# Attention and maxout FFN on one core: the order of every engine's work from a list scheduler in the source instead of the framework's

## The chip, the cores and the metric

One core of a Trainium2 chip runs the kernel. The metric is the device time of one execution in microseconds (us); the median of the runs is compared.

## The reference

Four batches, eight heads, 768 positions, head size 64. Each query sees only the keys that fall to the same of 16 centroids; the attention result, heads side by side, goes through a feed-forward layer whose hidden value is the largest of three products.

```python
q_assign = np.argmax(np.einsum('bhsd,hcd->bhsc', q_n, c_n), axis=-1)
k_assign = np.argmax(np.einsum('bhsd,hcd->bhsc', k_n, c_n), axis=-1)
mask = q_assign[:, :, :, None] == k_assign[:, :, None, :]
scores = np.where(mask, scale * np.matmul(q, k.transpose(0, 1, 3, 2)), -1000000000.0)
attn = np.exp(scores - np.max(scores, axis=-1, keepdims=True))
attn = attn / (np.sum(attn, axis=-1, keepdims=True) + 1e-09)
x = np.matmul(attn, v)                       # then (3072, 512), heads side by side
h = np.maximum(np.maximum(x @ w1, x @ w2), x @ w3)
out = h @ w_out
```

Operands are split into a high and a low 16-bit half, so each product is three or more TensorE passes.

## The kernel before

The unit of attention is a score tile: 128 queries of one head against all 768 keys. There are 192, numbered in this text from 1. `scores` makes one: four TensorE matmuls into a PSUM tile `big` (L505, L507), a scaled maximum on VectorE (L510), the exponential on ScalarE with the row's sum (L513), its high half on ScalarE (L515), its low half on VectorE for even steps and on GpSimd for odd ones (L517), and a transposing DMA of both halves into `pt` (L518), issued by SyncE like every other DMA of the kernel. On odd steps the exponential goes to a buffer `e` in SBUF, on even ones it stays in `big`.

Six tiles (three of each head of a pair) make a visit; 32 visits in all, 8 for each batch. After a visit `av_sums` (L526, L527, L532) spreads the inverse row sums into a `big` tile, `av` multiplies the transposed weights with V into it (36 matmuls, L540), and `x_split` (L551 to L558) scales it into the input `x16` of the FFN. For batches after the first the scaling (L553) needs `vrel`, which `v_common` (L309) forms when all four pairs of V of that batch have been scaled.

Four visits complete the 384 rows of one FFN block; there are eight. `hidden` makes 18 groups of 12 matmuls (L585), each taken from PSUM by ScalarE or VectorE (L595, L597); `outp` makes three groups of 18 (L619), taken by ScalarE (L628) and stored (L630). Both use PSUM tiles `one`.

Before its first visit a pair of heads is prepared: its load (L372), maxima (L381), a small power-of-two matmul (L390), the split into halves (L407 to L417), cluster scores on TensorE (L444, L448), copies between partitions (L424 to L427), and the one-hot cluster rows: a transpose, an addition, a subtraction and selections (L455 to L480), then four row DMAs into `qk` (L484). V is prepared in L344 to L352. In the first 230 us or so, 24 blocks of FFN weights are also loaded (L187), put together from halves (L194, L196), scaled by a power of two found with a small matmul (L102 to L111; the matmul is L106) and split (L205 to L207).

Buffers that matter here: three `big` and two `one` PSUM tiles; in SBUF four `hl`, three `pt`, two `e`, two `wd`, four `stage`, one `xs`.

The order: the source calls these functions step by step, gives each call a priority (`at_prio`, `spread`, `paced`, `put`) and some edges (`issue_after`), and the framework's scheduler, with a timing model of its own, orders single instructions by priority. The result is a fixed order on each engine; at run time an engine's head instruction waits for its semaphores, and what stands behind it waits too.

Of the kernel before, what the change touches and what calls it, by code (L numbers as in the profile page):

```python
# [9 lines left out]
F32R = mybir.dt.float32r  # L10
# [10 lines left out]
CSC = 2.0**10  # L21


@with_exitstack
def kernel(
# [11 lines left out]

# [13 lines left out]
    NG = QT // G  # L62

    cpool = ctx.enter_context(tc.tile_pool(name="const", bufs=1))
    sb = ctx.enter_context(tc.tile_pool(name="sb", bufs=2))
    ps_big = ctx.enter_context(tc.tile_pool(name="ps_big", bufs=3, space=PSUM))
    ps_one = ctx.enter_context(tc.tile_pool(name="ps_one", bufs=2, space=PSUM))

    def big():
        return ps_big.tile([P, 2 * 512], F32, tag="big", name="big")  # L70

    def one():
        return ps_one.tile([P, 512], F32, tag="one", name="one")

    def stage():
        return sb.tile([P, S], F32, tag="stage", name="stage", bufs=4)

    fp = [ctx.enter_context(tc.tile_pool(name="ffn", bufs=2))]
    tctx = ExitStack()
    tp = tctx.enter_context(tc.tile_pool(name="first", bufs=1))  # L80
    ident = cpool.tile([P, P], F32, name="ident")
    make_identity(nc, ident)
    ident16 = cpool.tile([P, P], BF16, name="ident16")
    nc.gpsimd.tensor_copy(ident16, ident)
    rank = cpool.tile([P, C], F32, name="rank")
    for c in range(C):
        nc.gpsimd.memset(rank[:, c : c + 1], float(C - c))
    onehot2 = cpool.tile([P, S // 32, 2, C], F16, name="onehot2")
    cw = cpool.tile([P, H, P], F16, name="cw")
    nc.gpsimd.memset(cw, 0.0)  # L90
    ksel = cpool.tile([P, 1], F32, name="ksel")
    for g in range(4):
        nc.gpsimd.memset(ksel[32 * g : 32 * g + 32], float(g & 1))
    hsel = cpool.tile([P, 2], F32, name="hsel")
# [3 lines left out]

    def pow2_scale(cols, name, p=None):

        m = sb.tile([P, 1], F32, tag="sc_m", name="sc_m", bufs=2)
        nc.vector.tensor_reduce(m, cols, axis=AX.X, op=ALU.max)  # L102
        nc.vector.tensor_scalar_max(m, m, 1e-30)
        nc.vector.tensor_scalar(m.bitcast(I32), m.bitcast(I32), 0x7F800000, None, op0=ALU.bitwise_and)
        a = one()[:, 0:P]
        nc.tensor.matmul(a, m.bitcast(BF16)[:, 1:2].broadcast_to([P, P]), ident16, start=True, stop=True)  # L106
        p = cpool.tile([P, 1], F32, name=f"p_{name}") if p is None else p
        s = sb.tile([P, 1], F32, tag="sc_s", name="sc_s", bufs=6)
        nc.vector.tensor_reduce(p, a, axis=AX.X, op=ALU.max)  # L109
        nc.vector.reciprocal(s, p)  # L110
        nc.vector.tensor_scalar_mul(s, s, 2.0**14)  # L111
        return p, s
# [3 lines left out]
    last = {}  # L116

    def behind(what, f, *args):
        with tc.issue_after(last[what].ins):
            f(*args)  # L120


    def load_centroids():
        c_sb = sb.tile([P, D], F32, tag="c_sb", name="c_sb", bufs=1)
        nc.sync.dma_start(out=c_sb, in_=cent)
        return c_sb

    def centroids(c_sb):
        warm = cpool.tile([P, 1], F32, name="warm")
        nc.vector.memset(warm, 1.0)  # L130
        nc.scalar.activation(warm, warm, AF.Sqrt)
        sq = tp.tile([P, D], F32, name="sq")
        ss = cpool.tile([P, 1], F32, name="c_ss")
        nc.vector.tensor_tensor(sq, c_sb, c_sb, op=ALU.mult)
        nc.vector.tensor_reduce(ss, sq, axis=AX.X, op=ALU.add)
        y0 = cpool.tile([P, 1], F32, name="c_y0")
        nc.scalar.activation(y0, ss, AF.Sqrt)
        nc.scalar.activation(warm, ss, AF.Exp)
        yr = cpool.tile([P, 1], F32, name="c_yr")
        nc.vector.tensor_scalar_max(yr, y0, 1e-18)  # L140
        nc.vector.reciprocal(yr, yr)
        nc.vector.tensor_tensor(yr, ss, yr, op=ALU.mult)
        nc.vector.tensor_tensor(yr, y0, yr, op=ALU.add)
        nc.vector.tensor_scalar(yr, yr, 0.5, 1e-6, op0=ALU.mult, op1=ALU.add)
        nc.vector.reciprocal(yr, yr)
        c2 = tp.tile([P, 2, D], F32, name="c2")
        cb = c_sb.rearrange("p (a d) -> p a d", a=1).broadcast_to([P, 2, D])
        nc.vector.tensor_scalar_mul(c2, cb, yr)
        t = one()
        nc.tensor.transpose(t[:, 0:P], c2.rearrange("p a d -> p (a d)"), ident)  # L150
        tv = t[:, 0:P].rearrange("p (h c) -> p h c", c=C)
        cv = cw.rearrange("p (r i) x -> p r i x", i=2)
        tv = tv.rearrange("p (r i) c -> p r i c", i=2)
        parts = []
        for a in range(2):
            rows = slice(D * a, D * a + D)
            for i in range(2):
                at = D * i + 32 * a
                parts.append((tv[rows, :, i, :], cv[rows, :, i, at : at + C], cv[rows, :, i, at + C : at + 2 * C]))
        for x, hi, lo in parts:  # L160
            last["cw_hi"] = nc.scalar.activation(hi, x, AF.Copy, scale=CSC)
        for x, hi, lo in parts:
            last["cw_lo"] = nc.vector.scalar_tensor_tensor(lo, x, CSC, hi, op0=ALU.mult, op1=ALU.subtract)

    JA = 4
# [34 lines left out]

    def w_units(wp, jt):
        mx = wmx[:, jt : jt + 1]  # L210
        n = CT * P
        got = {}

        def load(i):
# [599 lines left out]
```

## Time and profile before

| | us |
|---|---|
| three runs | 858.05, 856.37, 858.34 |
| median | 858.05 |
| the profiled execution's own time | 856.58 |
| its span | 854.8 |
| PE busy (matmuls) | 708.7 |
| DVE, ACT, POOL busy | 556.0, 474.2, 456.1 |
| granted TensorE clock over the span | 0.928 |

The span is the time between the first and the last recorded event of that execution, 1.78 us less than its own time. Engines: PE is TensorE, DVE VectorE, ACT ScalarE, POOL GpSimd, SP SyncE. L505 is line 505 of the kernel before. A row of waits reads: engine, tile and line that waited, what ended the wait, the total in us, how often, the longest.

### The profile page before, as it was taken

What the parts mean: (1) busy time and instruction counts of PE and PEld (TensorE: products, weight loads), DVE (VectorE), ACT (ScalarE), POOL (GpSimd) and SP (SyncE); (2) the same over time, 40 slices, a digit from 0 to 9 for tenths busy, and PEclk for the clock granted to TensorE, in tenths of its full rate; (3) what the DMA queues carried; (4) which work ended last, traced back from release to release, by engine and by line L of the source; (5) the groups of instructions that cost most, each with busy time, mean ns of one, the idle gap of its engine ahead of it and who ended that gap; (6) DMA issues with size and microseconds to landing.
All of it is one profiled execution on the core that took longest, in us unless ns stands there. A gap on an engine that the chain in (4) does not pass through costs nothing.

```text
span 854.8 us, 13244 instructions
## 1 busy us (share of the span) xinstructions
PE 708.7 (83%) x4629; PEld 390.5 (46%) x4629; DVE 556.0 (65%) x1150; ACT 474.2 (55%) x837; POOL 456.1 (53%) x448
## 2 busy tenths in 40 slices
PE   2254452667989999998987899999798999999997
PEld 1122121333555455554544455555345555555563
DVE  6967858879588486368675685569768764665020
ACT  5657555776754546564663566665457465566201
POOL 1267467498676544255873654366666643454221
PEclk9995665797999999999989999999899999999999
DMA  6698795899588766678977966688978976667300
GB/s 235 127 218 178 182 222 113 185 228 201 125 178 168 154 118 127 138 140 164 188 150 155 190 133 125 146 166 159 194 158 162 154 138 136 124 112 119 86 1 37
DMA packets 329154, 128.90 MB, mean 151 GB/s; under 512 B 304384, under 2 KB 315520, under 8 KB 329088
## 3 DMA queue, kind: packets, MB, share of 16 engines
q1 hardware_dynamic: 329088, 128.06, 72.4%
q8 instruction: 36, 0.59, 0.3%
q14 instruction: 30, 0.25, 0.1%
HBM read 31.49 MB, written 6.29 MB: 44 GB/s over the span
## 4 chain that ended last, share of the span: by engine, by line
PE 52%; DVE 16%; DMA 10%; POOL 9%; issue 7%; ACT 4%; SPq 1%; POOLq 0%; DVEq 0%; ACTq 0%
PE one L585 22%; PE one L619 10%; PE big L540 8%; DMA stage<-in_qk_dram 5%; PE big L505 4%; PE big L507 4%; DVE big L510 4%; PE big L532 2%; POOL hl L517 2%; DMA stage<-in_v_dram 2%; DMA wd<-in_moe_w_dram 2%; POOL qk L417 2%; DVE hl L517 2%; DVE wf L196 2%; DMA pt<-hl 1%
## 5 line engine op out<-in xcount | busy, mean ns | idle before, releaser
L517 POOL TENSOR_TENSOR hl<-e,hl 128x768 f16<-128x768 f32 x96 | 158.6, 1652 | 162.3 <-ACT hl L515 162.3
L510 DVE TENSOR_SCALAR_CACHE_REDUCE big<-big,nsc 128x768 f32<-128x768 f32 x192 | 193.8, 1019 | 63.3 <-PE big L507 61.7
L585 PE MATMUL one<-x,w16a 128*128 128x384 f16 x1152 | 207.7, 328 | 7.0 <-DVE vpow L109 3.2
L505 PE MATMUL big<-qk 128*128 128x512 f16 (+1 forms) x384 | 105.3, 358 | 65.8 <-ACT e L513 27.5
L513 ACT ACTIVATE big<-big,nm 128x768 f32<-128x768 f32 x96 | 83.9, 874 | 127.5 <-DVE big L510 103.3
L585 PEld LDWEIGHTS <-w16a 128*128 128x128 f16 x1152 | 110.8, 98 | 87.7 <-issue 18.0
L513 ACT ACTIVATE e<-big,nm 128x768 f32<-128x768 f32 x96 | 86.7, 903 | 74.7 <-DVE big L510 65.1
L540 PE MATMUL big<-pt,v 128*64 128x384 f16 x1152 | 118.6, 344 | 1.0 <-DMA pt<-hl 0.9
L507 PE MATMUL big<-qk 96*128 96x512 f16 (+1 forms) x384 | 107.0, 359 | 13.2 <-DMA qk<-cl_t 12.1
L517 DVE TENSOR_TENSOR hl<-big,hl 128x768 f16<-128x768 f32 x96 | 91.2, 950 | 33.7 <-ACT hl L515 33.7
L585 PE MATMUL one<-x,w16b 128*128 128x384 f16 x576 | 102.8, 329 | 0.0
L505 PEld LDWEIGHTS <-qk 128*128 128x128 f16 x384 | 36.0, 102 | 123.9 <-issue 91.6
L540 PEld LDWEIGHTS <-v 128*64 128x64 f16 x1152 | 72.8, 116 | 36.8 <-issue 10.1
L515 ACT CAST hl<-e 128x768 f16<-128x768 f32 x96 | 80.1, 835 | 1.6
L515 ACT CAST hl<-big 128x768 f16<-128x768 f32 x96 | 76.7, 799 | 1.8
L585 PEld LDWEIGHTS <-w16b 128*128 128x128 f16 x576 | 55.8, 98 | 39.8 <-issue 4.4
L557 POOL TENSOR_SCALAR x<-xs 128x384 f16<-128x384 f32 x32 | 16.8, 524 | 90.7 <-DVE xs L553 78.1
L507 PEld LDWEIGHTS <-qk 96*128 96x128 f16 x384 | 40.7, 106 | 46.3 <-DMA qk<-cl_t 12.0
L381 DVE TENSOR_REDUCE q_m<-stage 128x1 f32<-128x768 f32 x32 | 30.1, 948 | 40.9 <-DMA stage<-in_qk_dram 40.9
L619 PE MATMUL one<-wo,wf_h 128*128 128x512 f16 x216 | 50.9, 379 | 0.8 <-ACT o L628 0.8
L597 DVE SCALAR_TENSOR_TENSOR wf_h<-one,wf_h 128x384 f32<-128x384 f32 x48 | 26.4, 551 | 38.6 <-PE one L585 34.6
L417 POOL TENSOR_TENSOR qk<-stage,qk 128x768 f16<-128x768 f32 x30 | 49.4, 1656 | 0.9 <-ACT qk L416 0.8
(142 smaller groups left out, 927.8 us busy)
## 6 DMA issues: line engine op xcount, KB each, us to landing
stage<-in_qk_dram SPq DMA_DIRECT2D x32, 384.0 KB, 4.2
wd<-in_moe_w_dram SPq DMA_DIRECT2D x18, 512.0 KB, 4.9
out_dram<-o SPq DMA_DIRECT2D x24, 256.0 KB, 2.8
qk<-qk SPq DMA_DIRECT2D x15, 384.0 KB, 4.7
qk<-qk SPq DMA_DIRECT2D x30, 192.0 KB, 3.8
stage<-in_v_dram SPq DMA_DIRECT2D x12, 384.0 KB, 4.9
pt<-hl SPq DMA_TRANSPOSE x192, 4.0
wd<-in_moe_w_out_dram SPq DMA_DIRECT2D x6, 512.0 KB, 4.5
```

The source lines that it names most:

```text
L381: nc.vector.tensor_reduce(m2[:, i : i + 1], x, axis=AX.X, op=ALU.max, apply_absolute_value=True)
L417: last["lo"] = nc.gpsimd.tensor_tensor(t[:, AQ, i], x, t[:, BQ, i], op=ALU.subtract)
L505: nc.tensor.matmul(t[:, lo:hi], aq[:, qs], ak[:, lo:hi], start=True, stop=False)
L507: last["pe"] = nc.tensor.matmul(t[:, lo:hi], bq[0:K2, qs], bk[0:K2, lo:hi], start=False, stop=True)
L510: last["nm"] = nc.vector.tensor_scalar(e, e, nsc[b, h // 2], 3.0e38, op0=ALU.mult, op1=ALU.min, accum_out=nm)
L513: last["exp"] = nc.scalar.activation(x, e, AF.Exp, bias=nm, scale=-1.0, accum_out=r)
L515: nc.scalar.copy(hl[:, 0, :], x)
L517: eng.tensor_tensor(hl[:, 1, :], x, hl[:, 0, :], op=ALU.subtract)
L540: nc.tensor.matmul(t[D * i : D * i + D, 0:NB], v[:, i, kt, a], pts[i][:, :, c * QT + kt, :], start=(n == 0), stop=(n == len(parts) - 1),)
L585: nc.tensor.matmul(t[:, 0:NB], w16[jt // JA][:, jt % JA, wa, i, ct], x16[b, gi, ct][:, xa, :], start=(n == 0), stop=(n == 3 * CT - 1),)
L597: nc.vector.scalar_tensor_tensor(m, t[:, 0:NB], 2.0**-24, ms[jt], op0=ALU.mult, op1=ALU.max)
L619: nc.tensor.matmul(t[:, 0:DM], h16[jt][:, ha, tt * P : (tt + 1) * P], wo16[0][:, jt, wa, :], start=(n == 0), stop=(n == 3 * JT - 1),)
```

## The change

The framework's scheduling is switched off (`tc.manual_schedule()`), so that instructions stand in the order in which the source issues them. The source first collects every piece of work as a `Unit` (an engine, a cost in us, the units it depends on, the buffers that it leases, a priority), then `Plan.run` steps through a modelled time and gives each free engine the ready unit with the lowest priority number whose buffers are free, and issues it at once. A unit is a whole group: the four matmuls of a tile, all 36 of `av`, 12 or 18 of the FFN.

```diff
+class Plan:
+    LAG = {"PE": 0.17, "DVE": 0.085, "ACT": 0.09, "POOL": 0.03, "SP": 0.0}
+    SEM = 0.04
+    LAND = 1.45
+    RING = 2.6
+    AHEAD = 3.0
...
+                for u in ready[e]:
+                    if best is not None and (u.prio, u.n) >= (best.prio, best.n):
+                        continue
+                    when = can(u)
...
+                    if when > now + 1e-9:
+                        soonest = when if soonest is None else min(soonest, when)
+                        continue
+                    best = u
...
+                if e == "PE":
...
+                    cost = cost if warm else 2 * cost
...
+                if e == "SP":
+                    out = max(now + cost, server - self.RING)
+                    server = max(out, server) + u.work
+                    free[e] = out
+                    u.end = server + self.LAND
+                else:
+                    free[e] = now + cost
+                    u.end = now + cost + self.LAG[e] + u.tail
+                u.fn()
...
+    ctx.enter_context(tc.manual_schedule())
...
+        u = add("PE", 0.66, pe, u_qk[b, pr], [k, t], step)
+        u = add("DVE", 0.94, mx, [u, u_nsc[b, pr]], [t, nm], step, tail=0.06)
+        u = add("ACT", 0.88, exp, [u], list(dict.fromkeys([t, nm, rs, ex])), step, tail=0.02)
...
+        u_t.append(add("SP", 1.43, tr, [u], [hl, pt], step, work=2.15))
...
+    PREP_LEAD0 = (50, 12, 14, 14)
+    PREP_LEAD = 16
+    ROWS = (1, 1, 1, 1)
...
+    AV_PRIO = 0.5
+    F_0, F_SPAN = 3, 21
...
+    plan.run()
-    QK_BUFS = 4
-    QK_LO = (1, 0, 0, 0)
-    ROWS = (1, 0, 0, 0, 0)
...
-    AV_LAG = 2
-    PREP_LATE = -9
```

Every kind of instruction is issued as often as before, with two exceptions that follow from `ROWS`: the addition and the subtraction of the cluster rows (L461, L466; now L540, L549) run on VectorE for all four pairs of batch 0, where only the first pair had them there. Buffer counts and the visits' sequence are the same. Lines of the changed kernel: score tiles L909, L911 (PE), L915 (DVE), L931 (SP); `av` L855, L862; the division of x L875; FFN L967, L1019.

How the order moves, at three places. First TensorE, at the beginning. Before, behind the last matmul of tile 6: the small matmuls of pair 1 (`q_m`), of the first V and of the first weight block (both `sc_m`), a first matmul of the cluster scores of pair 1 (`cw`), then tile 7.

```order
L507 MATMUL big<-qk 128x256
L390 LDWEIGHTS q_m
L390 MATMUL one<-ident_78,q_m 128x128
L106 LDWEIGHTS sc_m
L106 MATMUL one<-ident_78,sc_m 128x128
L106 LDWEIGHTS sc_m
L106 MATMUL one<-ident_78,sc_m 128x128
L444 LDWEIGHTS cw
L444 MATMUL big<-qk,cw 64x512
L505 LDWEIGHTS qk
L505 MATMUL big<-qk 128x512
```

In the changed kernel the same engine, from the end of tile 5 to the beginning of tile 6:

```order
L911 MATMUL big<-qk 128x256
L317 LDWEIGHTS sc_m
L317 MATMUL one<-ident_80,sc_m 128x128
L909 LDWEIGHTS qk
L909 MATMUL big<-qk 128x512
```

Only the first V's matmul stands there; `q_m` of pair 1 stands ahead of tile 1, the cluster scores of pair 1 between tiles 2 and 3, and the first weight block's `sc_m` behind tile 9.

Second, the DMAs that SP issues at the beginning, before (`stage` and `in_qk_dram` are the loads of q and k, `vf` V of batch 0, `wd` weights, `pt<-hl` the transposes of score tiles):

```order
L372 DMA stage<-in_qk_dram 128x768 x2
L187 DMA wd<-in_moe_w_dram 128x4x512
L372 DMA stage<-in_qk_dram 128x768 x2
L320 DMA vf<-in_v_dram 128x1536 x2
L187 DMA wd<-in_moe_w_dram 128x4x512
L372 DMA stage<-in_qk_dram 128x768 x2
L518 DMA_TRANSPOSE pt<-hl 128x12x128
L187 DMA wd<-in_moe_w_dram 128x4x512
L518 DMA_TRANSPOSE pt<-hl 128x12x128 x2
L187 DMA wd<-in_moe_w_dram 128x4x512
```

And in the changed kernel:

```order
L628 DMA vf<-in_v_dram 128x1536 x2
L716 DMA wd<-in_moe_w_dram 128x4x512
L410 DMA stage<-in_qk_dram 128x768 x2
L716 DMA wd<-in_moe_w_dram 128x4x512
L515 DMA qk<-qk 64x2x1536
L410 DMA stage<-in_qk_dram 128x768
L518 DMA qk<-qk 64x1536
L410 DMA stage<-in_qk_dram 128x768
L520 DMA qk<-qk 64x1536
L931 DMA_TRANSPOSE pt<-hl 128x12x128 x2
L716 DMA wd<-in_moe_w_dram 128x4x512
```

The copies of pair 1 between partitions (`qk<-qk`) and two more loads now stand ahead of the first transpose; before, those copies stood behind tile 6.

Third, VectorE at the first visit of batch 1 (tiles 49 to 54). Before, behind the reciprocal of its row sums (`rs`) comes `cv` (what `vrel` points at) of batch 1, and two tiles later the division of its x (L553, outside this piece):

```order
L527 RECIPROCAL rs<-rs 128x6
L381 TENSOR_REDUCE q_m_3469<-stage 128x1
L309 TENSOR_SCALAR cv_2358<-vpow,iv_2356 128x4
L613 TENSOR_TENSOR so<-so,p_o 128x1 x2
L510 TENSOR_SCALAR big,nm<-big,nsc 128x768
```

In the changed kernel the reciprocal of that visit stands behind the maximum of tile 55, and `cv` and the division here, ahead of the maxima of tiles 66 and 67; the second L875 is the next visit's:

```order
L320 TENSOR_REDUCE vpow<-one 128x1
L321 RECIPROCAL sc_s<-vpow 128x1
L322 TENSOR_SCALAR sc_s<-sc_s 128x1
L681 TENSOR_REDUCE pv_133<-vpow 128x1
L682 RECIPROCAL iv_134<-pv_133 128x1
L683 TENSOR_SCALAR cv_135<-vpow,iv_134 128x4
L875 SCALAR_TENSOR_TENSOR xs<-big,cv_135,xs 128x384
L928 TENSOR_TENSOR hl<-big,hl 128x768
L981 SCALAR_TENSOR_TENSOR wf_h<-one,wf_h 128x384
L1005 TENSOR_TENSOR so<-pv_133,p_w 128x1 x2
L915 TENSOR_SCALAR big,nm<-big,nsc 128x768
L875 SCALAR_TENSOR_TENSOR xs<-big,cv_135,xs 128x384
```

So the first visit's result stays in its PSUM tile over some nine tiles more; in batches 2 and 3 it is six each.

More of the change, by code (lines that the diff above doesn't have):

```diff
@@ L21, with __init__, __call__ @@
 CSC = 2.0**10
+class Lease:
+    def __init__(self, plan, tag, make):
+        self.tag, self.make, self.users, self.held, self.tile = tag, make, [], False, None
+        plan.leases.append(self)
+    def __call__(self):
+        if self.tile is None:
+            self.tile = self.make()
+        return self.tile
+class Unit:
+    def __init__(self, eng, cost, fn, deps, leases, prio, tail, work):
+        self.eng, self.cost, self.fn, self.leases, self.prio = eng, cost, fn, leases, prio
+        self.deps = [d for d in deps if d is not None]
+        self.tail, self.work, self.end, self.next = tail, work, None, []
@@ L67 @@
     ps_one = ctx.enter_context(tc.tile_pool(name="ps_one", bufs=2, space=PSUM))
+    fp = ctx.enter_context(tc.tile_pool(name="ffn", bufs=2))
+    first_ctx = ExitStack()
+    first = first_ctx.enter_context(tc.tile_pool(name="first", bufs=1))
+    caps = {
+        "big": 3, "one": 2, "stage": 4, "e": 2, "hl": 4, "pt": 3, "rs": 3, "v16": 4, "qk": 4,
+        "x16_0": 4, "x16_1": 4, "xs": 1, "wd": 2, "wf": 2, "vf": 2, "nm": 6, "cl_t": 1, "top": 1,
+        "sc_m": 3, "sc_s": 6, "q_s": 2, "w_s": 2,
+    }
@@ L97 @@
     nc.gpsimd.memset(hsel[D:P, 1:2], 1.0)
[L99 to L112, printed above, removed]
@@ L116 @@
[L116 to L129, printed above, removed]
-        nc.vector.memset(warm, 1.0)
[L131 to L151, printed above, removed]
@@ new lines, with warm_up @@
+    c_sb = const([P, D], F32, "c_sb")
+    u_c = add("SP", 0.58, lambda: nc.sync.dma_start(out=c_sb, in_=cent), prio=-50, work=0.3)
+    def warm_up():
+        nc.vector.memset(warm, 1.0)
+    u_w = add("DVE", 0.06, warm_up, prio=-50)
+    u_w = add("ACT", 1.5, lambda: nc.scalar.activation(warm, warm, AF.Sqrt), [u_w], prio=-50)
+    sq = first.tile([P, D], F32, name="sq")
+    c2 = first.tile([P, 2, D], F32, name="c2")
+    ss = const([P, 1], F32, "c_ss")
+    y0 = const([P, 1], F32, "c_y0")
+    yr = const([P, 1], F32, "c_yr")
@@ L158, in centroids @@
                 at = D * i + 32 * a
[L159 to L173, printed above, removed]
-    w16 = [cpool.tile([P, JA, 2, 3, CT, P], F16, name="w16a")]
-    wo16 = []
-    wcol = cpool.tile([P, JT], F32, name="wcol")
@@ L289, in common, with resc @@
+        wsc["w"], wsc["o"] = pw, po
+        u = wsc["u"] = plan.chain("DVE", comm, [u] + [x for jt in range(JT) for x in u_w16[jt][:1]], [s], prio)
+        for jt in range(JT):
+            def resc(jt=jt):
                 t = wo16[0][:, jt].rearrange("p a n -> p (a n)")
                 nc.scalar.activation(t, t, AF.Copy, scale=r[:, jt : jt + 1])
-            wsc["w"], wsc["o"] = pw, po
-        return [load(jt) for jt in range(JT)], [part(jt) for jt in range(JT)], common
-    vmax = cpool.tile([P, B, NPAIR], F32, name="vmax")
```

1217 lines of the change are left out of this document (717 added, 500 removed).

## The prediction

> **What bounds the kernel now.** I read the page first, for the chain that ended last and the DMA queue:
>
> ```profile
> span 854.8 us, 13244 instructions
> PE 52%; DVE 16%; DMA 10%; POOL 9%; issue 7%; ACT 4%; SPq 1%; POOLq 0%; DVEq 0%; ACTq 0%
> q1 hardware_dynamic: 329088, 128.06, 72.4%
> ```
>
> TensorE (PE) carries half of the chain, but no engine carries it alone, and the one queue that SP feeds keeps the 16 DMA engines busy for 72.4% of the span. An average over such a span hides its stages, so I cut it next. The windows give busy time of each engine (number of instructions), granted clock and DMA share; the cuts lie at tiles 1, 49, 73, 97, 121, 145, 169 and at the last ones:
>
> ```profile
> core 0: us, PE busy (x) PEld busy (x) DVE busy (x) ACT busy (x) POOL busy (x), PEclk, DMA share, GB/s
> 0.00:21.00 21.00, 5.24 (x17) 2.02 (x18) 13.69 (x37) 11.37 (x15) 3.35 (x32) 1.00 0.66 239
> 21.00:235.00 214.00, 118.94 (x695) 59.24 (x694) 162.68 (x350) 140.06 (x238) 136.84 (x120) 0.77 0.81 178
> 235.00:340.00 105.00, 101.47 (x680) 57.11 (x677) 76.01 (x155) 54.46 (x98) 59.35 (x56) 0.98 0.73 150
> 340.00:431.00 91.00, 84.54 (x566) 47.68 (x565) 57.72 (x119) 50.30 (x91) 50.63 (x47) 0.96 0.80 159
> 431.00:530.00 99.00, 89.70 (x602) 50.48 (x602) 65.78 (x145) 54.16 (x99) 55.32 (x51) 0.96 0.75 150
> 530.00:621.00 91.00, 83.75 (x574) 46.58 (x573) 64.04 (x130) 52.84 (x95) 51.62 (x48) 0.96 0.81 163
> 621.00:706.00 85.00, 81.16 (x572) 46.29 (x570) 61.02 (x121) 51.73 (x95) 51.81 (x48) 1.00 0.80 151
> 706.00:788.00 82.00, 82.00 (x568) 47.49 (x567) 45.69 (x83) 49.21 (x92) 33.40 (x33) 1.00 0.70 126
> 788.00:855.00 67.00, 61.91 (x369) 33.59 (x366) 9.39 (x17) 10.04 (x18) 13.79 (x18) 1.00 0.16 42
> ```
>
> Three regimes. Up to 235 us (batch 0, the weights) nothing is full: DVE 76% of the second window, the DMA engines 81%, PE 56% at a clock of 0.77. From 235 to 788 PE is nearly full; from 706 to 788, where nothing more is prepared, it is full at full clock, and that stage is my yardstick: 82.00 us for 568 matmuls, 0.1444 us each. After 788 the last FFN block runs on PE almost alone.
>
> What an order can give back is waiting. By the yardstick the five stages from 235 to 706 should have taken 680, 566, 602, 574 and 572 times 0.1444, that is 98.2, 81.7, 86.9, 82.9 and 82.6 us; they lost 6.8, 9.3, 12.1, 8.1 and 2.4, together 38.7 us. Of these PE stood idle for 30.4 (the five windows, 471.0, less the busy times, 440.6); the rest went with the lower clock.
>
> The Trainium skill ("Perfetto Trace Analysis", Identifying the Most-Contended Engine) says that busy matmul time tells little of how near TensorE is to its limit, and that the busy share of weight loads tells more. By the weight loads (47.49 in 82.00) the same five stages lost 42.6 instead of 38.7, and the steady term below would be 16.7 instead of 15.2; the trace agrees in order of size.
>
> Next the waits of PE. In the first regime (20 to 235 us) the largest are
>
> ```profile
> PE big L505 <- ACT e L513: 23.4, 8, 6.8
> PE one L106 <- DVE sc_m L104: 15.4, 5, 8.0
> PE big L444 <- ACT qk L416: 14.8, 4, 9.7
> PE big L507 <- DMA qk<-cl_t: 12.1, 2, 8.9
> ```
>
> and from 230 to 807
>
> ```profile
> PE big L505 <- DVE cl_t L455: 5.6, 1, 5.6
> PE big L505 <- ACT e L513: 4.1, 4, 2.5
> PE big L505 <- DVE sc_m L102: 3.2, 1, 3.2
> PE one L585 <- DVE vpow L109: 3.2, 1, 3.2
> ```
>
> The second to fourth rows of the first view are instructions standing at the head of PE's queue before their input exists (a power-of-two matmul, cluster scores of a later pair, a tile whose cluster rows have not landed), with ready score tiles behind them. The same on SP, whose transposes wait at the head for their low half with loads behind them:
>
> ```profile
> SPq L518 <- POOL hl L517: 29.6, 7, 15.9
> SPq L518 <- DVE wf L196: 10.9, 2, 9.9
> SPq L424 <- ACT qk L416: 7.5, 2, 6.0
> ```
>
> In slices of 10 us the DMA engines swing between empty and full accordingly:
>
> ```profile
> 20.00:30.00 10.00, 3.51 (x10) 1.49 (x11) 9.72 (x15) 6.00 (x10) 1.64 (x1) 1.00 0.00 1
> 40.00:50.00 10.00, 3.22 (x10) 1.27 (x10) 4.25 (x17) 6.13 (x9) 7.31 (x7) 1.00 1.08 242
> 90.00:100.00 10.00, 4.83 (x16) 2.02 (x16) 9.86 (x27) 4.57 (x8) 3.69 (x5) 0.67 0.53 129
> 130.00:140.00 10.00, 2.87 (x8) 0.94 (x7) 10.00 (x16) 7.22 (x14) 8.54 (x8) 0.50 0.38 92
> ```
>
> **The change, part by part.** *Same work.* Every instruction stays but for two cluster-row operations of three pairs, which go from POOL to DVE. They and two pieces of the PE chain, from the chain in order of time:
>
> ```profile
> 14.97 0.57 DVE cl_t L461
> 16.15 0.57 DVE cl_t L466
> 60.15 0.85 POOL cl_t L466
> 214.94 1.95 PE one L585 x12
> 741.36 3.04 PE big L540 x35
> ```
>
> DVE gets 3 x (0.57 + 0.57) = 3.4 us more, POOL loses some 3 x 2 x 0.85 = 5.1. In the first 235 us DVE is idle for 58.6 and each pair's chain gets shorter by 0.28 or more per operation: I cost it at nothing; without that cover it is +3.4.
>
> *Batch 0.* The 173 us of DMA (0.81 x 214), 163 of DVE and 119 of PE in that window are all still to be done, so the stage cannot shrink below about 173 by this alone; its idle DMA time is 40.7 us. What moves in the order speaks for less waiting: two of the three matmuls that held up tile 7 have left that place, the cluster scores of pair 1 come ahead of tile 3, the rows of pair 1 are sent behind tile 4 instead of 8, and more transfers stand ahead of the first transpose, where DMA lay empty for 10 us. Against it: the first transpose now stands behind a copy that needs pair 1's cluster scores, and so does every load behind it; and a fixed order by another model will have misplacements of its own. No row shows what is left over. The bounds: at best the waits of rows two to four of the first PE view (42.3 us) cost as much as DMA idleness and most of the 40.7 comes back, say 34; at worst nothing comes back and the new head-of-queue waits cost a wait of the old size, 15.4, more. I take a third of the idle DMA time, 14: nearer to the middle than to the best, because DVE, at 76%, is the next to be full, and after 14 us less it would be at 83%.
>
> *FFN begun earlier.* Counted in the order, 13 hidden groups stand ahead of tile 48's end against 11 before. PE has idle time there and little later, so 2 x 1.95 = 3.9 us of PE work leave the full stages. If PE has no idle time there: nothing.
>
> *Batches 1 to 3.* PE's order hardly differs in kind: 36 hidden groups lie between tiles 38 and 71, where they lay between 34 and 71. What differs is when a batch's preparation is sent: the four row groups of batch 2 go out behind tiles 82, 87, 96 and 102, where they went behind 86, 95, 100 and 109, for pairs needed at tiles 97, 103, 109 and 115. Cluster scores, power-of-two matmuls and row landings are the waits of the second PE view, so these should shrink. I give back half of the idle 30.4, that is 15.2, and leave the clock as it is. Bounds: all of 38.7, and none with the price of the next paragraph.
>
> The Trainium skill ("TensorE: Matmul & The Clock Gate", Part 1) says that the clock falls to half after an idle window of some 3.4 us and rises after as long a busy one. By that rule shorter waits would also return half of the 8.3 us lost with the clock, and the time would be 4 less. The trace agrees in part: 1.00 in 706 to 788 without waits, 0.96 in the stage with the 5.6 us wait, but also 0.98 in 235 to 340.
>
> *New waits.* `av` comes later behind its visit: counted over the 32 visits, 4.1 tiles on the mean against 3.1. And the first visits of batches 1 to 3 keep their PSUM tile nine, six and six tiles longer, since the division waits for the last V of the batch. Behind them on PE stand the next scores, which need a `big` tile. How long a tile is held:
>
> ```profile
> L510 DVE TENSOR_SCALAR_CACHE_REDUCE big<-big,nsc 128x768 f32<-128x768 f32 x192 | 193.8, 1019 | 63.3 <-PE big L507 61.7
> L513 ACT ACTIVATE big<-big,nm 128x768 f32<-128x768 f32 x96 | 83.9, 874 | 127.5 <-DVE big L510 103.3
> L515 ACT CAST hl<-big 128x768 f16<-128x768 f32 x96 | 76.7, 799 | 1.8
> L517 DVE TENSOR_TENSOR hl<-big,hl 128x768 f16<-128x768 f32 x96 | 91.2, 950 | 33.7 <-ACT hl L515 33.7
> ```
>
> An even tile needs 1.02 + 0.87 + 0.80 + 0.95 = 3.6 us after its matmuls. The windows of L510 alone (two records for each tile) show how often one comes:
>
> ```profile
> 340.00:431.00 91.00, 25.48 (x48) 0.96 0.80 159
> ```
>
> That is 24 tiles in 91 us, one in 3.8. Two buffers take a tile in about 1.8 at best, so two suffice unless waits double the holding: 0, with 46 (the rival below) as the other end.
>
> *The tail.* The last 18 hidden and 3 output groups stay behind the last visit, and the output groups of the block before still fill the wait for the last transposes: 0.
>
> *The sum*, against the profiled execution's own 856.58 us (span 854.8 and 1.78 around it): 856.58 - 14 - 3.9 - 15.2 = 823.5. The median of the runs shown, 858.05, is 1.5 above that execution, which gives 825.0.
>
> **The rivals.** *Most of the waiting goes:* 30 in batch 0, 3.9, and 34 of the 38.7: 856.6 - 67.9 = 788.7, 790 with the 1.5. For it: the DMA engines can be above 1.0 in a slice, and PE is full in 706 to 788. Against it: a fixed order needs slack somewhere, and the preparing stages want 0.80 of DMA and up to 72% of DVE besides PE. Chance 0.18.
>
> *The waits only move:* the old and the new order are both lists made by a model, the PE order is alike from batch 1 on, and in-order queues wait wherever the model is wrong. 850 to 861, worked out as no term at all: 858. For it: the rival lists agree in the steady part to within a tile or two. Chance 0.12, half of it within 0.3%.
>
> *PSUM becomes the bound at the batch starts* (slower). While one of three `big` tiles is kept for 9 + 6 + 6 = 21 tiles, the others must turn around; if waits of DVE and ACT stretch a tile to 12 us, two buffers give one tile in 6 instead of 3.8, and the FFN groups between don't fill PE: 21 x 2.2 = 46 us, and with all the gains of the sum 823.5 + 46 + 1.5 = 871. It begins at a stretch to 7.6 us, twice the tile's pace, and turns the sign at 10.8 (33.1 / 21 = 1.6 us a tile more, twice). Chance 0.10.
>
> *Transposes wait for `av`* (slower). Three `pt` buffers hold a visit and a half, so the transpose of a visit's fourth tile waits at the head of SP's queue until the last visit's `av` is done. In the order `av` stands four tiles or more behind its visit in 25 visits, where it did in 10. If each of the 15 more stops the queue for an `av` of 3.04 us on a path that counts, 46 us: 823.5 + 46 + 1.5 = 871. Against it: DMA is at 0.73 to 0.81 there, so such a stop can be made up. It turns the sign above 2.2 us a visit (33.1 / 15). Chance 0.10.
>
> **How the numbers follow.** The forecast, 825, with its own range of 805 to 845, has what is left, 0.50. A measurement of this kernel can tell about 0.3% from no change. Faster: 0.50 + 0.18 + 0.04 of the third case = 0.72; within 0.3%: 0.06; slower: 0.02 + 0.20 = 0.22. For eight in ten the range must reach most of the 790 case and the no-change case, and some of the slow ones: 786 to 864.
>
> **What would show it.** Right: tile 49 near 220 us instead of 235; a DMA share above 0.85 from 21 us to there; the slice 20 to 30 not empty; PE idle between there and the last tile near 15 us; the waits L106, L444 and L507 of the first view smaller. Wrong: waits of the scores (now L909) on the division of x or the low half would show the PSUM rival, waits of SP's transposes on `av` (now L862) the other; and if the steady stages keep 0.1444 us x count + 39 us, the forecast's third term was never there.

## The result, and the profile after

| | before | after |
|---|---|---|
| median of four runs of each on one chip, us | 857.21 | 827.16 |
| their range | 855.92 to 858.34 | 826.0 to 833.62 |
| the profiled execution's own time and span | 856.58, 854.8 | 827.95, 826.1 |
| PE busy, granted clock over the span | 708.7, 0.928 | 696.1, 0.934 |

The ratio is 0.9665, with a 95% interval of 0.9612 to 0.9718: the change made the kernel 30 us faster. The forecast was 825.0. But the 30 us did not come from where the forecast took them: batch 0 gave none of its 14, and the rest gave 29 where 19 were forecast. The two errors cancel, so the closeness of the total is luck.

From the page of the changed kernel, the chain that ended last and the DMA queue:

```profile
span 826.1 us, 13236 instructions
PE 57%; DVE 21%; issue 7%; ACT 7%; POOL 5%; DMA 3%; SPq 0%; DVEq 0%; ACTq 0%; POOLq 0%
q1 hardware_dynamic: 329088, 128.06, 75.9%
```

The same transfers, a larger part of the chain on PE (57% for 52%) and a smaller one on DMA (3% for 10%). The windows, cut at the same places as those of before to within one tile:

```profile
21.00:235.00 214.00, 130.08 (x742) 68.22 (x743) 176.16 (x359) 136.18 (x233) 134.47 (x116) 0.78 0.81 178
235.00:335.00 100.00, 93.41 (x639) 53.13 (x638) 69.83 (x145) 54.50 (x99) 56.09 (x52) 0.98 0.80 160
335.00:427.00 92.00, 87.83 (x616) 50.28 (x615) 67.42 (x131) 54.78 (x100) 59.80 (x56) 1.00 0.88 172
427.00:514.00 87.00, 80.15 (x565) 47.93 (x563) 66.29 (x138) 50.58 (x91) 49.94 (x46) 0.98 0.81 155
514.00:600.00 86.00, 83.99 (x600) 49.40 (x598) 66.02 (x125) 54.61 (x100) 58.03 (x53) 1.00 0.96 184
600.00:685.00 85.00, 81.11 (x559) 46.38 (x558) 58.26 (x125) 50.21 (x90) 46.23 (x43) 0.96 0.73 140
685.00:759.00 74.00, 73.49 (x536) 44.35 (x534) 43.21 (x79) 46.76 (x88) 33.43 (x32) 1.00 0.77 140
759.00:826.00 67.00, 62.66 (x373) 34.15 (x371) 9.43 (x18) 9.95 (x18) 13.05 (x17) 1.00 0.15 36
```

The cut at 235 us is where the maximum of tile 48 begins, the last of batch 0, in both kernels (234.8 before, 234.7 after); the forecast calls this cut tile 49. So batch 0 takes the same 214 us at the same DMA share of 0.81. From there to the last tile's maximum it is 524 us (235 to 759) where it was 553 (235 to 788). The tail is 67 in both. So the gain lies behind that cut. Some 5 us of it lie right at it: the maximum of tile 49 follows at 240.4 us in the kernel before and at 235.6 in the changed one, and whoever cuts there counts them with batch 0.

Inside batch 0 the new order is ahead for a long time. The changed kernel's maxima alone (L915; two records for each tile, then clock, DMA share, GB/s):

```profile
21.00:118.00 97.00, 24.05 (x46) 0.78 0.86 191
118.00:145.00 27.00, 6.26 (x12) 0.56 0.73 160
145.00:185.00 40.00, 6.49 (x13) 0.67 0.87 196
185.00:235.00 50.00, 12.85 (x25) 0.97 0.70 147
```

and those of the kernel before (L510) in the same windows:

```profile
21.00:118.00 97.00, 21.45 (x40) 0.75 0.81 175
118.00:145.00 27.00, 4.29 (x8) 0.63 0.71 170
145.00:185.00 40.00, 12.51 (x24) 0.79 0.87 189
185.00:235.00 50.00, 11.86 (x23) 0.86 0.83 177
```

At 145 us 29 tiles are done against 24. In the next 40 us the changed kernel does 6.5 and the kernel before 12, and the lead is gone. No engine is full in those 40 us; the row of all engines is

```profile
145.00:185.00 40.00, 22.66 (x134) 12.18 (x133) 27.57 (x61) 21.95 (x38) 25.69 (x24) 0.67 0.87 196
```

The waits of PE, first from 20 to 235 us, then from 230 to 780:

```profile
PE big L909 <- ACT e L921: 23.4, 9, 6.3
PE big L909 <- DVE hl L928: 20.8, 6, 9.1
PE one L317 <- DVE sc_m L307: 11.5, 6, 3.0
PE big L855 <- ACT e L921: 7.8, 3, 6.2
```

```profile
PE big L909 <- ACT e L921: 5.5, 7, 2.2
PE one L431 <- DVE q_m L425: 5.3, 3, 2.0
PE big L502 <- POOL qk L476: 4.4, 5, 1.3
PE one L967 <- DVE wf_h L981: 2.8, 1, 2.8
```

In batch 0 the waits for cluster scores (14.8) and for row landings (12.1) are gone from the head of the list, the power-of-two matmul went from 15.4 to 11.5, and in their place stands the wait of the next scores for a `big` tile (the second row, 20.8, was 10.6 before; the first was 23.4 before too). From 230 on, the longest wait is 2.8 us where it was 5.6.

### The profile page after: what moved, and what is told of

Same layout as the page of the kernel before. It is cut to its first block, busy times and chain, and to the rows that moved or that the text cites. A ratio compares the mean times of both kernels' runs of the same rounds, so it can differ in the third digit from the quotient of the medians.

```text
span 826.1 us, 13236 instructions
## 1 busy us (share of the span) xinstructions
PE 696.1 (84%) x4629; PEld 395.3 (48%) x4629; DVE 572.3 (69%) x1156; ACT 472.6 (57%) x837; POOL 456.3 (55%) x442
## 4 chain that ended last, share of the span: by engine, by line
PE 57%; DVE 21%; issue 7%; ACT 7%; POOL 5%; DMA 3%; SPq 0%; DVEq 0%; ACTq 0%; POOLq 0%
PE one L967 25%; PE big L862 11%; PE one L1019 9%; DVE big L915 5%; PE big L909 4%; PE big L911 4%; PE big L855 3%; DVE hl L928 2%; ACT e L921 2%; ACT hl L924 2%; DVE cl_t L555 1%; DVE onehot L566 1%; DMA pt<-hl 1%; POOL hl L928 1%; DVE wf L724 1%
## 5 line engine op out<-in xcount | busy, mean ns | idle before, releaser
L928 POOL TENSOR_TENSOR hl<-e,hl 128x768 f16<-128x768 f32 x96 | 160.9, 1676 | 149.1 <-ACT hl L924 144.6
L915 DVE TENSOR_SCALAR_CACHE_REDUCE big<-big,nsc 128x768 f32<-128x768 f32 x192 | 192.9, 1018 | 29.3 <-PE big L911 27.7
L967 PE MATMUL one<-x,w16a 128*128 128x384 f16 x1152 | 202.6, 331 | 4.9 <-DVE wf_h L981 2.8
L909 PE MATMUL big<-qk 128*128 128x512 f16 (+1 forms) x384 | 105.4, 360 | 62.2 <-ACT e L921 26.7
L967 PEld LDWEIGHTS <-w16a 128*128 128x128 f16 x1152 | 113.1, 99 | 85.8 <-issue 14.7
L911 PE MATMUL big<-qk 96*128 96x512 f16 (+1 forms) x384 | 106.3, 361 | 5.4 <-DVE qk L591 5.4
L862 PE MATMUL big<-pt,v 128*64 128x384 f16 x1152 | 108.6, 346 | 1.4 <-ACT xs L871 1.3
L967 PE MATMUL one<-x,w16b 128*128 128x384 f16 x576 | 99.5, 326 | 0.4 <-DVE vpow L320 0.4
L862 PEld LDWEIGHTS <-v 128*64 128x64 f16 x1152 | 73.4, 117 | 30.0 <-issue 4.0
L909 PEld LDWEIGHTS <-qk 128*128 128x128 f16 x384 | 35.9, 103 | 100.1 <-issue 64.0
L967 PEld LDWEIGHTS <-w16b 128*128 128x128 f16 x576 | 55.9, 97 | 38.4 <-issue 1.3
L911 PEld LDWEIGHTS <-qk 96*128 96x128 f16 x384 | 41.0, 107 | 37.9 <-issue 10.9
L875 DVE SCALAR_TENSOR_TENSOR xs<-big,cv,xs 128x384 f32<-128x384 f32 x24 | 14.7, 612 | 52.5 <-ACT xs L871 37.7
L871 ACT COPY xs<-big 128x384 f32<-128x384 f32 x32 | 15.4, 480 | 61.8 <-PE big L862 58.4
L1019 PE MATMUL one<-wo,vf_h 128*128 128x512 f16 x216 | 49.2, 385 | 0.6 <-DVE q_p L435 0.6
```

The lines of the kernel that those rows point to most:

```text
L862: nc.tensor.matmul(t()[D * i : D * i + D, 0:NB], v()[:, i, kt, a], pts[i]()[:, :, c * QT + kt, :], start=(m == 0), stop=(m == len(parts) - 1),
L909: nc.tensor.matmul(t()[:, lo:hi], aq[:, qs], ak[:, lo:hi], start=True, stop=False)
L911: nc.tensor.matmul(t()[:, lo:hi], bq[0:K2, qs], bk[0:K2, lo:hi], start=False, stop=True)
L915: nc.vector.tensor_scalar(s, s, nscs[:, b, pr : pr + 1], 3.0e38, op0=ALU.mult, op1=ALU.min, accum_out=nm())
L928: eng.tensor_tensor(hl()[:, 1, :], e(), hl()[:, 0, :], op=ALU.subtract)
L967: nc.tensor.matmul(t()[:, 0:NB], w16[jt // JA][:, jt % JA, wa, i, ct], x16[b, gi, ct]()[:, xa, :], start=(m == 0), stop=(m == 3 * CT - 1),)
```

## The experiments

In each, the edit is one to the changed kernel unless the text says otherwise. The table gives the median, the ratio to runs of the kernel before on the same chip, and two stretches of the trace of one execution: the end of batch 0, cut where the maximum of tile 48 begins, and the time from there to the last tile's maximum with PE's busy time in it. Each kernel has one trace, and executions of one kernel differ by 2 to 9 us, so a few us between two stretches say little.

| run | median us | ratio, 95% interval | tile 48 at | to the last tile, PE busy |
|---|---|---|---|---|
| before | 857.21 | 1 | 235 | 553, 522.6 |
| after | 827.16 | 0.9665 (0.9612 to 0.9718) | 235 | 524, 500.0 |
| e1_framework | 831.12 | 0.9725 (0.9675 to 0.9775) | 223 | 544, 506.4 |
| e2_rows | 826.65 | 0.9658 (0.9615 to 0.9702) | 235 | 525, 499.9 |
| e3_av_early | 835.34 | 0.976 (0.9713 to 0.9806) | 229 | 539, 502.4 |
| e4_prep_late | 816.15 | 0.9538 (0.9501 to 0.9576) | 230 | 517, 496.1 |
| e5_dma_free | 863.63 | 1.0089 (1.0056 to 1.0122) | 232 | 564, 514.6 |
| e6_source_order | 1408.89 | 1.6454 (1.6394 to 1.6514) | 429 | 913, not cut |
| e7_weights_early | 822.62 | 0.9615 (0.9571 to 0.9659) | 237 | 513, 492.0 |
| e8_weights_late | 824.68 | 0.9625 (0.959 to 0.966) | 230 | 526, 500.1 |
| e9_filler | 816.55 | 0.9536 (0.9483 to 0.959) | 229 | 517, 495.2 |
| e10_warm_plan | 821.39 | 0.9595 (0.9556 to 0.9634) | 236 | 518, 499.3 |
| e11_prep_later | 849.97 | 0.9921 (0.9896 to 0.9946) | 229 | 551, 508.8 |
| e12_short_max | 809.71 | 0.9463 (0.9444 to 0.9482) | 225 | 516, 494.3 |

**The framework's scheduler on the new source.**

```diff
-    ctx.enter_context(tc.manual_schedule())
```

> The changed kernel with the framework's scheduling left on: the list scheduler's order is then only the sequence in which instructions are issued and so their priority, and the framework's own timing model decides the order on each engine. Theory (the gain comes from the order that the list scheduler fixes with durations taken from the chip): most of the gain is lost, 845 to 865 us, and PE's waits between 235 us and the last tile are back above 25 us. Rival (it is the priorities and whole groups of the new source that help, whoever orders them): within 1% of the changed kernel, 820 to 835.

Measured: 831.12 us. The sequence in which the plan issues the work still goes into the framework's scheduler, which now moves instructions within it. The windows of batch 0 and of the rest up to the last tile:

```profile
21.00:223.00 202.00, 125.81 (x742) 65.40 (x743) 174.97 (x356) 138.96 (x235) 136.17 (x116) 0.80 0.87 189
223.00:767.00 544.00, 506.39 (x3504) 289.44 (x3503) 360.11 (x743) 310.80 (x567) 300.60 (x278) 0.98 0.78 152
```

By the total the rival is right: the time is 0.5% from that of the changed kernel, and the intervals of the two ratios overlap. The theory's sign came all the same, PE's idle time in the steady part is 37.6 us (544 less 506.4) where the changed kernel has 24.0. For the two parts of the span go opposite ways: batch 0 ends 12 us earlier than in the changed kernel (the DMA share is 0.87 for 0.81), and the steady part takes 20 us more (544 for 524, for the same number of matmuls). Cut at tile 49's own maximum (227.7 us here), these are 8 and 16; and this trace is of the longest of the four executions, 5 us above their median. So the plan's sequence carries most of the gain even here (24 us below the 854.94 of the kernel before on the same chip); holding to it exactly gains some 16 to 20 us in the steady part and loses 8 to 12 in batch 0.

**The rows back on GpSimd.**

```diff
-    ROWS = (1, 1, 1, 1)
+    ROWS = (1, 0, 0, 0)
```

> The changed kernel with the cluster rows of pairs 1 to 3 of batch 0 back on GpSimd for the addition and the subtraction, as before the change; the list scheduler orders the rest anew. Theory (this move is a side show; the order is the change): 822 to 832. Rival (VectorE, 98% busy from 21 to 69 us in the changed kernel, is what holds batch 0): 3.4 us less on VectorE brings tile 48 forward, 817 to 824. A third way (the shorter chain is what gains): slower, 832 to 840.

Measured: 826.65, 0.5 us from the changed kernel, and the same stretches to 1 us. The one exception to "same work" is worth nothing.

**`av` earlier behind its visit.**

```diff
-    AV_PRIO = 0.5
+    AV_PRIO = -3.0
```

> The changed kernel with the attention-times-V group of each visit given a priority 3.5 tiles earlier, so that it stands nearer behind its visit, as before the change. Theory (its place costs little in the steady stages, where transposes have slack): 822 to 834. Rival (transposes wait for it at the head of the DMA queue, and its PSUM tile is kept from the scores): faster by 5 to 20 us, 807 to 822. Slower than 834 would say that an early group waits on PE for its last transposes with ready work behind it.

Measured: 835.34, 8 us slower (the intervals just meet). Tile 48 comes 6 us earlier, and the rest takes 15 more. The reason named for this case does not show: of PE's waits of 0.4 us and more from 229 us on, none is `av` waiting for its transposes. `av` late behind its visit was the condition of the prediction's second slower rival, and that rival's sign is there in the changed kernel, where the kernel before has no such row:

```profile
SPq L931 <- PE big L862: 12.2, 9, 2.5
```

With `av` earlier these waits of the transposes fall to 2.9 us, and the steady part becomes longer: the waits exist, but they do not hold the time.

**The preparation of a batch later.**

```diff
-    PREP_LEAD = 16
+    PREP_LEAD = 10
```

> The changed kernel with the preparation of each pair of batches 1 to 3 given a priority 10 tiles ahead of its first visit instead of 16. Theory (sending the next batch's preparation early is what removes the waits of batches 1 to 3): 835 to 850, with waits of scores for cluster rows between 235 us and the last tile. Rival (the lead is not what matters; the balance of engines is): 823 to 832.

Measured: 816.15, 11 us faster than the changed kernel, and the intervals do not meet. The steady part:

```profile
230.00:747.00 517.00, 496.07 (x3510) 289.73 (x3509) 369.79 (x748) 310.35 (x570) 301.46 (x278) 0.99 0.84 161
```

and its largest waits:

```profile
PE big L909 <- DVE hl L928: 7.6, 7, 2.1
PE big L909 <- ACT e L921: 3.9, 5, 1.9
```

Both expectations are missed on the fast side. With this lead the four row groups of batch 2 go out behind tiles 88, 94, 101 and 108, that is about where the kernel before sent them (86, 95, 100, 109). The steady gain does not go away with that; it grows. The forecast's reason for it, "the preparation is sent earlier", is refuted.

**Later still.**

```diff
-    PREP_LEAD = 16
+    PREP_LEAD = 6
```

> The changed kernel with a preparation lead of 6 steps instead of 16 (10 gave 816.15 us). Theory A, the later the preparation the less it stands in the way of the score tiles, as from 16 to 10: 806 to 814, with a loss of PE time from tile 48 on of under 12 us. Theory B, 10 is near the best, and at 6 the first visits of a batch wait for their cluster rows: waits of the scores on row landings of over 3 us at the starts of batches 1 to 3, loss above 20, 820 to 832.

Measured: 849.97, outside both ranges. At 6 almost all of the gain is gone, but not by waits for row landings as expected (PE has no such wait of 0.7 us or more). The two rows below stood at 7.6 and 3.9 with a lead of 10:

```profile
PE big L909 <- DVE hl L928: 18.5, 11, 3.2
PE big L909 <- ACT e L921: 10.2, 8, 2.2
```

The scores wait for a `big` tile. That fits a preparation that has become urgent and stands ahead of the low halves on VectorE, but no run separated this. Leads of 16, 10 and 6 give 827, 816 and 850: this one setting moves the time by up to 34 us.

**The model of the DMA queue switched off.** The plan takes every transfer as landed when it is issued, and any number may be under way: the landing time, the time of the transfer itself and the limit go together.

```diff
-    LAND = 1.45
-    RING = 2.6
+    LAND = 0.0
+    RING = 1e9
...
-                    u.end = server + self.LAND
+                    u.end = out
```

> The changed kernel, its list scheduler told that a DMA has landed as soon as it is issued and that DMAs never queue (landing time 0, no limit on what is outstanding). Only the order changes. Theory (what helps in batches 1 to 3 is that work is placed by durations taken from the chip): the loss of PE from tile 49 on goes from 21 us back to 35 or more, 840 to 855 us. Rival (priorities by tile number do it, and the durations matter little): 820 to 834.

Measured: 863.63, beyond the theory's range and 0.9% slower than the kernel before. Batch 0 hardly changes (232), the steady part takes 564, and PE's largest waits there are

```profile
PE big L862 <- DMA pt<-hl: 13.4, 4, 4.7
PE one L317 <- DVE wf_h L981: 10.9, 2, 6.1
PE big L909 <- DVE hl L928: 7.5, 5, 3.3
```

The first did not stand among the waits of the changed kernel: `av` now stands on PE before its transposes have landed, and what is behind it waits. This single part of the model carries more than the whole steady gain (40 us of stretch against 29).

**Source order without a scheduler.** The kernel before, with its edges left out, its instructions in the order of its source.

```diff
+    ctx.enter_context(tc.manual_schedule())
...
-        with tc.issue_after(last[what].ins):
-            f(*args)
+        f(*args)
...
-                for k in keys:
-                    st.enter_context(tc.issue_after(last[k].ins))
-                u()
+            u()
```

> The kernel before with the framework's scheduling switched off and the edges between calls left out, so that instructions stand in the order in which its steps call them, group by group. Theory (a planned order is needed, and whole groups alone do not give it): slower than before, 900 to 1050 us. Rival (the framework's reordering of single instructions is what cost the kernel before its time): 825 to 850.

Measured: 1408.89, slower as expected, but far beyond the range. PE's waits over the span:

```profile
PE one L107 <- DVE sc_m L105: 247.6, 20, 20.6
PE big L532 <- DVE rs L527: 222.5, 32, 26.0
PE one L390 <- DVE q_m L384: 99.7, 12, 15.4
```

The same instructions and buffers, 1.65 times the time. The 32 waits of the second row are the 32 visits: each stops PE until its row sums are done, and what other steps have ready stands behind it in the queue.

**The weights earlier, and later** (both with a lead of 10).

```diff
-    W_0, W_STEP = 3, 1.5
+    W_0, W_STEP = -2, 1.4
```

> The changed kernel with the late preparation of the run before (a lead of 10 tiles instead of 16) and the FFN weights 5 tiles earlier at 1.4 instead of 1.5 tiles a block. Theory (batch 0 is held by VectorE and by PSUM tiles that are kept, while the FFN could begin earlier): tile 48 stays near 230 us, more of the FFN is done by then, 805 to 814 us. Rival (weights ahead of the first tiles push the tiles back by their own work): 816 to 826.

```diff
-    W_0, W_STEP = 3, 1.5
+    W_0, W_STEP = 3, 1.8
```

> The same late preparation with the FFN weights spread wider, 1.8 instead of 1.5 tiles a block. Theory as for the run with early weights: tile 48 comes some 10 us earlier since less of VectorE's work stands between the tiles, but as much FFN work is left over, 812 to 822 us. Rival (the crowding of batch 0 with weights costs more than it saves): 800 to 810.

Measured: 822.62 and 824.68, against 816.15; the first lies in its rival's range, the second above both of its ranges. Earlier weights bring batch 0 to 237 and the rest to 513; later ones leave batch 0 at 230 and the rest takes 526. Neither shortens batch 0.

**TensorE kept busy in batch 0** (with a lead of 10). Five matmuls behind the scores of tiles 9 to 37, last in priority; nobody uses their results.

```diff
+    for k in range(8, 37):
+        for i in range(5):
+            t = one()
+
+            def fill(t=t):
+                nc.tensor.matmul(t(), cw[:, 0, :], cw[:, 0:4, :], start=True, stop=True)
+
+            add("PE", 0.22, fill, [u_pe[k], u_cw], [t], 900 + k)
```

> The changed kernel with the preparation lead of 10, and five more matmuls of 128x512 behind the scores of each of the tiles 9 to 37, lowest in priority, whose results nobody uses (145 matmuls added). In the lead-10 run (816.15 us) tile 48 ended at 230 us although TensorE was busy for some 120 of the 209 us before; its clock there was about 0.6 and an av took 4.7 to 5.2 us where it takes 3.04 later. Theory A, the half clock holds batch 0: with the fillers the clock there is above 0.9, av is near 3.1, tile 48 ends at 210 to 220 and the time is 798 to 808. Theory B, batch 0 is held by VectorE and the PSUM turn-around and TensorE is not on its path: the clock rises too, but tile 48 stays at 228 to 240 and the time at 815 to 826, the fillers costing a little where they stand in the way. 808 to 815 would be a part of both.

Measured: 816.55, and tile 48 at 229. Batch 0 of the run with a lead of 10:

```profile
21.00:230.00 209.00, 126.64 (x738) 67.38 (x739) 176.13 (x349) 135.24 (x231) 134.04 (x116) 0.72 0.84 183
```

and with the fillers:

```profile
21.00:229.00 208.00, 150.43 (x884) 77.10 (x884) 174.62 (x351) 134.77 (x231) 131.21 (x115) 0.90 0.84 182
```

The clock rose from 0.72 (the expectation had put it at about 0.6) to 0.90 and 24 us of matmuls found room, and nothing came of it. So the half clock of TensorE does not hold batch 0, unless the fillers cost as much by standing in the way as the clock gave; no run separates the two.

**The plan without a cold clock** (with a lead of 10).

```diff
-                    cost = cost if warm else 2 * cost
+                    cost = cost
```

> The changed kernel with the preparation lead of 10, and the plan takes every TensorE unit at its full-clock duration, also after idle time, where it doubled it. Theory A, the order's worth rests on durations that are right on every engine: the plan is now wrong in batch 0 alone, where the clock is low, so tile 48 ends 5 to 12 us later (235 to 242) and the time is 821 to 828. Theory B, only the landing times of the DMAs matter (without them the time went from 827 to 864), TensorE's doubling does not: 813 to 820, tile 48 at 227 to 234.

Measured: 821.39; tile 48 at 236 where it was 230. The size is that of the first theory, and it lies in batch 0, where it should. The intervals of the ratios meet at their edges (0.9556 to 0.9634 against 0.9501 to 0.9576), so the 5 us is likely, not certain.

**Less work on VectorE in batch 0** (with a lead of 10). The same order, but three kinds of maxima read 64 columns; most of the search for the largest value is left out.

```diff
-    nc.vector.tensor_reduce(o, xs[i](), axis=AX.X, op=ALU.max, apply_absolute_value=True)
+    nc.vector.tensor_reduce(o, xs[i]()[:, 0 : (S if b else 64)], axis=AX.X, op=ALU.max, apply_absolute_value=True)
...
-    vmax[:, 0, i : i + 1], x[i](), axis=AX.X, op=ALU.max, apply_absolute_value=True
+    vmax[:, 0, i : i + 1], x[i]()[:, 0:64], axis=AX.X, op=ALU.max, apply_absolute_value=True
...
-    nc.vector.tensor_reduce(mx, x(), axis=AX.X, op=ALU.max, apply_absolute_value=True)
+    nc.vector.tensor_reduce(mx, x()[:, 0:64], axis=AX.X, op=ALU.max, apply_absolute_value=True)
```

> The kernel with a preparation lead of 10, in the same order of instructions, but three maxima of batch 0 on VectorE read 64 columns instead of all: those of q and k (768 columns, 0.94 us each, eight of them), of the first V (1536, 1.75 us, two) and of the weight blocks (1536, 1.75 us, six). So it leaves out most of the search for the largest value; the powers of two may come out smaller. VectorE loses some 18 us of its 176 us of work between 21 and 230 us, nothing else changes. Theory A, VectorE holds batch 0 (46.6 of 48 us busy from 21 to 69, 43.4 of 48 from 69 to 117, 176 of 209 in all): tile 48 comes 10 to 18 us earlier, at 212 to 220, and the time is 797 to 807. Theory B, the DMA queue and the waits of SP behind each other hold it (DMA share 0.84, up to 0.91): tile 48 at 226 to 231, time 812 to 818. 807 to 812 would be a part of both.

Measured: 809.71, between the two theories, tile 48 at 225:

```profile
21.00:225.00 204.00, 129.33 (x740) 68.62 (x740) 163.50 (x350) 135.32 (x231) 133.06 (x116) 0.78 0.86 187
```

VectorE lost 12.6 us of work in batch 0 (176.13 to 163.50), not the 18 expected, and batch 0 became 5 us shorter: some 40% of what was taken came through. VectorE is a part of what holds batch 0, neither all of it nor nothing.

## Why the prediction was right in its total

**Batch 0, 14 us: failed.** "I take a third of the idle DMA time" came to nothing: 214 us and a DMA share of 0.81 before and after. The waits it counted on did shrink, and others took their place. The step that failed is the price of a wait: the idle DMA time was taken as the measure of what waiting cost, with the next limit set by VectorE at 83%. The experiments bound what holds batch 0. It is hardly TensorE's clock (e9: nothing), not the weights' position (e7, e8: nothing gained), and VectorE's work only in part (e12: 5 of 12.6 us). The order has a part: e1 has the same instructions and ends batch 0 at 223, with DMA shares of 1.04 and 0.99 where the changed kernel has 0.73 and 0.87:

```profile
118.00:145.00 27.00, 15.51 (x83) 7.89 (x83) 19.83 (x39) 19.84 (x36) 22.86 (x22) 0.63 1.04 215
145.00:185.00 40.00, 27.72 (x181) 15.26 (x180) 38.02 (x81) 27.59 (x50) 27.43 (x25) 0.80 0.99 227
```

So 8 to 12 us for a better order of the same work were there to be had, and the plan's own order missed them. Which of its placements between 145 and 185 us does it stays open; a visit of some 40 us stands there in the changed kernel and, with a lead of 10, one later (tiles 37 to 42).

**FFN begun earlier, 3.9 us: right, but larger.** In the steady stretch, before and then after, the hidden matmuls are

```profile
L585 PE MATMUL one<-x,w16a 128*128 128x384 f16 x888 | 161.6, 328 | 6.0 <-DVE vpow L109 3.2 <-ACT wf_h L595 2.1 <-DVE q_m L384 0.6
L585 PE MATMUL one<-x,w16b 128*128 128x384 f16 x504 | 91.0, 329 | 0.0
```

```profile
L967 PE MATMUL one<-x,w16a 128*128 128x384 f16 x864 | 153.4, 331 | 3.8 <-DVE wf_h L981 2.8 <-POOL x L890 1.0
L967 PE MATMUL one<-x,w16b 128*128 128x384 f16 x492 | 85.5, 326 | 0.4 <-DVE vpow L320 0.4
```

That is 1392 and 1356, 36 fewer: three groups of 12 left the stretch, not two, or 5.9 us at 1.95.

**Batches 1 to 3, 15.2 us: right in place and sign, too small, and for another reason.** The stretch shrank by 29 us, 23 without those groups. By the forecast's own yardstick, the 2979 matmuls of the five stages from 235 to 685 should take 430.2 us at 0.1444; they took 450, a loss of 19.8 where it was 38.7, so 18.9 came back. "Half of the idle 30.4" is not how it came. Idle time of PE in the stretch went from 30.4 to 24.0 (524 less 500.0), 6.4 us; the other 22.7 are busy time, of which the three groups are 5.9. "I leave the clock as it is" is one miss: by the windows' clocks the five stages lost 13.3 us of clock before (105 x 0.02 + 91 x 0.04 + 99 x 0.04 + 91 x 0.04) and 7.1 after (100 x 0.02 + 87 x 0.02 + 85 x 0.04), 6.2 us. The other shows in `av`, before and after:

```profile
L540 PE MATMUL big<-pt,v 128*64 128x384 f16 x864 | 85.8, 332 | 1.0 <-DMA pt<-hl 0.9
```

```profile
L862 PE MATMUL big<-pt,v 128*64 128x384 f16 x864 | 75.0, 326 | 1.4 <-ACT xs L871 1.3
```

The same 864 matmuls, each as long as before to 2%, took 10.8 us less of busy time. A part of that is only counting: the records of pipelined matmuls overlap, and a group's busy time holds each of its records in full, also where another line's matmuls already run. Counted in the trace from each start to the next on PE, idle time left out, the 864 take 81.4 and 72.9 us, 8.5 less. The trace also shows where most of these lie. The changed kernel issues each `av` as a whole; the framework took all but one of these 24 apart, mostly with the first matmul alone and other work between. One visit before, then one after (start, duration, what):

```profile
654.33 0.33 PE L540 MATMUL big<-pt,v 128*64 128x384 f16 x1
659.73 3.11 PE L540 MATMUL big<-pt,v 128*64 128x384 f16 x35
```

```profile
636.00 3.12 PE L862 MATMUL big<-pt,v 128*64 128x384 f16 x36
```

In the stretch 24 `av` stand in 57 pieces before and in 24 after. From an `av` matmul to one of another line it took 0.23 us before and 0.24 after on the mean, to the next of `av` 0.084 and 0.080. So the 33 pieces more cost an estimated 33 x 0.15, or 5 us, of the 8.5. The clock is not the main part: in the last full stages, both at 1.00, the 144 `av` matmuls were busy for

```profile
706.00:788.00 82.00, 13.69 (x144) 1.00 0.70 126
```

before and for 12.45 us after: 1.2 us less, where a stage has 1.8 less on the mean. So the forecast's idle time was not all that an order could give back. The 6.2 of the clock and the 8.5 of `av` overlap in part and are not to be added up, and no run changed the splitting of `av` alone.

The reason given, that preparation is sent earlier, is wrong (e4). What the runs put in its place: the plan's model of the DMA queue is needed, since without it the order is worse than the framework's (e5), and so is holding to the order, since an order that lets the framework move instructions loses 16 to 20 us in the steady part (e1). Neither is enough: with the same durations a lead of 6 steps loses nearly all of the gain (e11). Beyond this, which of the plan's placements make the steady part shorter stays open.

**The clock.** The prediction set a rule of the Trainium skill ("TensorE: Matmul & The Clock Gate", Part 1: half clock after an idle window of some 3.4 us) beside the sum, worth 4 us more; by the windows the clock gave 6.2. The rows agree with it in part: the longest wait of PE went from 5.6 to 2.8 us and the clock of two of the five stages rose to 1.00. They also speak against it as a full account, since the stage from 600 to 685 has a clock of 0.96 and its longest wait is

```profile
PE one L431 <- DVE q_m L425: 2.0, 1, 2.0
```

The half clock is granted there twice, at 604.5 and 618.1 us, and in the 3.4 us ahead of it PE was idle for 2.0 and 1.6 us.

**What was costed at nothing.** The row operations: right (e2). The tail: right (67 us, before and after).

**The rivals.** "The waits only move" came true for batch 0 and for it alone. "Most of the waiting goes" did not come with this change; with a lead of 10 the kernel stands at 816, between the forecast and that rival's 790. PSUM as the bound: its sign, scores waiting for a `big` tile, stands there in batch 0 (23.4 us, as before the change, and 20.8, for 10.6 before), but it was priced for the starts of batches 1 to 3, and from 230 us on the larger of these rows is 5.5 us in all, so it decided nothing there. Transposes waiting for `av`: its sign came (12.2 us on SP), but taking the waits away made the kernel slower (e3), so they are not what the rival priced at 46 us.

**The signs named.** Batch 0 ending near 220, a DMA share above 0.85 and PE idle near 15 did not come: 235, 0.81, and 24.0. The slice from 20 to 30 us did fill, from a DMA share of 0.00 to 0.59, and the waits on L106, L444 and L507 did go down, and bought nothing: that step can be seen right in every sign of its waits and still fail in its time.

## What to carry to other kernels

Removing the waits at the head of a queue in a stage where no engine is full says little about that stage's time, since others take their place: look for the stage where one engine is nearly full, and count there. A list order written into the source rests on its durations, and here first of all on its model of the DMA queue (864 us without it, 827 with it); take the durations from the trace, and try the lead of a prefetch in both directions, since 16, 10 and 6 steps gave 827, 816 and 850 us here. When a scheduler is replaced, run the new source under the old scheduler too: it tells the source's share from the scheduler's, by stage.

## What the runs showed that was not expected

An engine without idle time can still lose time to its order: splitting `av` into 57 pieces instead of 24 cost an estimated 5 us, which no row of waits shows, since a step from an `av` matmul to one of another line took some 0.15 us more than one within `av` and stayed below the length of a record (0.33). TensorE's clock in batch 0 could be brought from 0.72 to 0.90 by 24 us of matmuls that nobody needs without a microsecond's change in the time. And the best run that leaves nothing out is neither kernel of this case: the changed one with a lead of 10 steps, 816.15 us, 4.6% below the kernel before.
